# Moving a chunk's combining work on VectorE and ScalarE behind the next cell's normalisation

## The chip, the cores and the metric

The kernel runs on one core of a Trainium2 chip. Its time is the device time of one execution in microseconds (us), and a kernel's time is the median over its runs. A core has a matrix engine (PE, with its weight loads shown apart as PEld), a vector engine (DVE), a scalar engine (ACT), GpSimd (POOL) and a queue engine that issues DMAs (SP). Every engine works through its own instructions in the order in which the program wrote them, and waits for the others by semaphores.

## The reference

An mLSTM cell with exponential gating is followed by a two-layer block whose activation is h·cos(h). Everything is float32 on the chip (the two weight matrices come as float64).

```python
batch, n_heads, seq, head_dim = (4, 8, 768, 40)
n_tokens, d_model, d_ff = (3072, 320, 2048)

for t in range(S):                       # the cell, per batch b and head h
    m_new = max(f_gate + m, i_gate)
    f_stab, i_stab = exp(f_gate + m - m_new), exp(i_gate - m_new)
    C = f_stab * C + i_stab * outer(v, k);  n = f_stab * n + i_stab * k
    y[t] = sigmoid(o_gate) * (C @ q) / max(abs(n @ q), 1)
x = y.transpose(0, 2, 1, 3).reshape(B * S, H * D)     # 3072 x 320
h = x @ w_in                                          # 3072 x 2048
out = (h * cos(h)) @ w_out                            # 3072 x 320
```

## The kernel before

**Tiling.** The sequence is cut into NC = 6 chunks of 128 steps. A *cell* `n = c*B + b` is chunk c of batch b (B = 4, 24 cells). Within a cell the recurrence is done in parallel form: decays `E` (exponentials on ACT, L402), scores (`ps`, PE, L468), weighting (DVE, L474), values (`vt`, PE, L494 to L501), and a running state `st` between chunks. `turn_gate` (L446) and `normalize_turned` (L510 to L521) on DVE multiply by the output gate, divide by the normaliser and write the cell's columns of `xT`; `seam` (L569, L576) on PE then turns the last rows of that (`px`) and makes the state's update (`pu`).

The block works on one chunk of all four batches at a time, 512 tokens. Its 2048 hidden columns go in eight *slots* f2 = 0..7 of 2 x 128 columns. In a slot, PE makes `pup` (two PSUM banks, L611 and L614); ACT rounds it (`near`, L619), DVE takes the rest (L622), ACT makes the sine (L627), DVE makes the gated value `g` (`gate`, L631), and DVE and POOL form sums of quarters of `g` (`sums`, L680 to L688). Only two `pup` banks exist, so a slot's first matmul waits until the slot before it has been through `gate`.

From chunk 1 on the product with w_out uses a scheme with seven products in place of eight. Each chunk has four accumulators `acc` = X0, X1, Y0, Y1 in PSUM (pool `ps_o`, four banks in rotation). The last twelve products of chunk c-1 run in slot 0 of chunk c; the remaining two products per slot pair are kept as operands `D` and run in slot 1 of chunk c as `late`, 16 matmuls (32 records) that go into a fifth accumulator, which takes the bank that X0 had. `combine(c, p)` (L730 to L748) puts the accumulators together: for each p, one ACT copy of `X[:, 0]` into a scratch tile `m` (L737), then DVE additions (L738 to L748), and for p = 0 two output DMAs. `combine_late` (L750) adds `late` and sends the other two outputs. The scratch `m` has one buffer, shared (tag "db") with `db` of the normalisation; the second copy of a pair therefore waits for the additions that read the first.

**Order.** The program is written under a manual schedule: `both_parts(c, b)` (L924) writes two slots at a time, and each engine runs what it is given in that order. While the block works on chunk c, the cells of chunk c+1 run between its slots: in the first slot of a pair (i = 0) scores, weighting, decay of the next cell, values, normalisation; in the second (i = 1) `seam` and state. `down_slot` (L761) places the products. The end of a slot with i = 0 is `sin_next` (L914): a sine on a single element, which makes ACT load the table for sines ahead of the next slot. In slot 0 of a chunk `sigmoid` of the next chunk and `decay` stand on ACT ahead of that. `late_products` and `combine_late` stand in slot 1.

SP issues its DMAs in program order too: in slot 0 the two output DMAs of `combine`, and the load of a later cell's `E` (`load_E`, L351).

The slot 0 that matters is called the *seam of chunk c* below (c = 2, 3, 4). For c = 5 there is no next cell, so the block `if cell and i == 0` is skipped.

Of the kernel before, what the change touches and what calls it, by code (L numbers as in the profile page):

```python
# [29 lines left out]
def kernel(  # L30
# [430 lines left out]
    def scores(n):  # L461
        pool, tag = psum(n)
        qT, kT = qkT[n]
        ps = [pool.tile([128, HP, C], FP, name="ps", tag=tag) for _ in range(2)]
        for p in range(HP):
            for j in range(2):
                r = slice(64 * j, 64 * j + D)
                nc.tensor.matmul(ps[j][:, p], kT[r, p], qT[r, p], start=True, stop=True)  # L468
        pss[n] = ps
# [165 lines left out]
    def down(c, f2):  # L635
        if f2 == 0:
            po[c] = [ps_o.tile([128, DM], FP, name="po", tag="o") for _ in range(B)]

        order = [(f, b) for f in (2 * f2, 2 * f2 + 1) for b in range(B)]
        if f2 == NF // 2 - 1:  # L640
            order.sort(key=lambda fb: fb[1])
        for f, b in order:
            nc.tensor.matmul(po[c][b], gs[c, f][:, ts(b, C)], w_out_sb[:, f], start=(f == 0), stop=(f == NF - 1))  # L643
            if f == NF - 1:
                o = out_tile()
                nc.scalar.copy(out=o, in_=po[c][b])
                out_to(c, b, o)
# [5 lines left out]
    def out_tile():  # L653
        return po_s.tile([128, DM], FP, name="o_sb", tag="o_sb")

    def out_to(c, b, o):
        nc.sync.dma_start(out=out[b * S + c * C:b * S + (c + 1) * C], in_=o)
# [54 lines left out]
    def late_products(c):  # L712
        L = late[c] = ps_o.tile([128, 2, HALF], FP, name="late", tag="o")
        for k in range(NF // 2):
            for i, rhs in ((0, wv[:, k, 0, 1]), (1, wv[:, k, 1, 1])):
                yield L[:, i], Ds[c, k // 4][:, k % 4, i], rhs, k == 0 and i == 0, k == LAST and i == 1

    def run(made, n):
        for _ in range(n):
            a, lhs, rhs, start, stop = next(made)  # L720
            nc.tensor.matmul(a, lhs, rhs, start=start, stop=stop)  # L721

    def all_products(c):
        acc[c] = [ps_o.tile([128, 3, HALF], FP, name="acc", tag="o") for _ in range(4)]
        if c == NC - 1:
            late[c] = ps_a.tile([128, 2, HALF], FP, name="late", tag="a")
        for k in range(NF // 2):
            yield from products(c, k)

    def combine(c, p):  # L730

        X0, X1, Y0, Y1 = acc[c]
        X, Y, y = (X0, Y0, (0, 1)) if p == 0 else (X1, Y1, (0, 1))
        tt = nc.vector.tensor_tensor
        o = outs_of[c, p] = [out_tile() for _ in range(2)]
        s = p1.tile([128, 3 * C], FP, name="m", tag="db")
        nc.scalar.copy(out=s[:, 0:HALF], in_=X[:, 0])  # L737
        tt(out=o[0].rearrange("q (h n) -> q h n", h=2), in0=X[:, 1:3], in1=s[:, 0:HALF].unsqueeze(1).to_broadcast([128, 2, HALF]), op=OP.add)  # L738
        if p == 0:
            tt(out=s[:, HALF:DM], in0=Y[:, 0], in1=o[0][:, HALF:DM], op=OP.add)  # L740
            tt(out=o[1].rearrange("q (h n) -> q h n", h=2), in0=Y[:, 1:3], in1=s[:, HALF:DM].unsqueeze(1).to_broadcast([128, 2, HALF]), op=OP.add)
            tt(out=o[0][:, HALF:DM], in0=Y[:, 2], in1=o[0][:, HALF:DM], op=OP.add)
            tt(out=o[0][:, HALF:DM], in0=Y1[:, 2], in1=o[0][:, HALF:DM], op=OP.add)
            for e in range(2):
                out_to(c, e, o[e])
        else:
            tt(out=o[1][:, HALF:DM], in0=Y[:, 0], in1=o[0][:, HALF:DM], op=OP.add)
            tt(out=o[1][:, 0:HALF], in0=Y[:, 1], in1=o[1][:, HALF:DM], op=OP.add)  # L748

    def combine_late(c):  # L750
        tt = nc.vector.tensor_tensor
        o, L = outs_of[c, 1], late[c]
        tt(out=o[0][:, HALF:DM], in0=L[:, 0], in1=o[0][:, HALF:DM], op=OP.add)
        tt(out=o[1][:, HALF:DM], in0=L[:, 0], in1=o[1][:, HALF:DM], op=OP.add)
        tt(out=o[0][:, HALF:DM], in0=L[:, 1], in1=o[0][:, HALF:DM], op=OP.add)
        for e in range(2):
            out_to(c, 2 + e, o[e])
# [3 lines left out]
    def down_slot(c, f2):  # L761

        if c == 0:
            if f2 > 0:
                down(0, f2 - 1)
            return
        if f2 == 0:
            if c == 1:
                down(0, LAST)
            else:  # L770
                run(made_of[c - 1], 12)
                combine(c - 1, 0)
                combine(c - 1, 1)
            return
        if f2 == 1 and c > 1:
            run(late_products(c - 1), NF)
            combine_late(c - 1)
            return
        if c not in made_of:
            made_of[c] = all_products(c)  # L780
        each = 14 if c == NC - 1 else 12
        quota = [0] * 8
        for m in range(2, 8):
            quota[m] = each * 7 * (m - 1) // 6 - each * 7 * (m - 2) // 6
        run(made_of[c], each if c == 1 else quota[f2])
# [128 lines left out]
    def sin_next():  # L914

        nc.scalar.activation(out=spot, in_=spot, func=AF.Sin)
# [7 lines left out]
    def both_parts(c, b):  # L924

        n = (c + 1) * B + b
        cell = n < N
        for i in range(2):
            f2 = 2 * b + i
            up = Up(c, f2)  # L930
            if cell and i == 0:
                scores(n)
                if c == 0 and b == 0:

                    warm(8, psum_o())
            if cell and i == 1:
                seam(n)
                if n % 2 == 1 and n + 3 < N:
                    load_two(n + 3, "Kv")
            for e in range(2):  # L940
                up.near(e)
            for e in range(2):
                up.rest(e)
            if i == 0:
                if cell:
                    weigh(n)
                    if n + 1 < N:
                        decay_exponents(n + 1)
                for e in range(2):
                    up.sin(e)  # L950
                    up.gate(e)
                if c > 0:
                    sums(c, f2)
                if b == 0 and c + 1 < NC:
                    sigmoid(c + 1)

                if c == 0 and b > 0 and pieces:
                    to_float32(*pieces.pop(0))
                if cell and n + 1 < N and (c > 0 or b > 0):
                    decay(n + 1)  # L960
            else:
                if cell:
                    seam_out(n)
                if pieces:
                    to_float32(*pieces.pop(0))
                if cell:
                    state(n)
                for e in range(2):
                    up.sin(e)
                    up.gate(e)  # L970
                if c > 0:
                    sums(c, f2)
                while pieces:
                    to_float32(*pieces.pop(0))
                if cell and n + 1 < N:
                    weigh_k(n + 1)
                    odd_values(n + 1)
            down_slot(c, f2)
            if (c, f2) == (1, 0):
                weight_sums(1)  # L980
            if cell and i == 0:
                turn_gate(n)
                values(n)
                normalize_turned(n)
                fade(n)
                if n % 2 == 1 and n + 3 < N:
                    load_two(n + 3, "qk")
                if n + 3 < N:
                    load_E(n + 3)
                if b == B - 2 and c + 2 < NC:  # L990
                    load_o(c + 2)
                if c == 0 and b == 0:
                    next_out()
                    decay(n + 1)
                elif pieces:
                    to_float32(*pieces.pop(0))
                sin_next()
            if i == 1:
                if c == 0 and b + 2 < B:
                    pieces.extend(weights_in(b + 2))  # L1000
                for _ in range(min(2, len(outs))):
                    next_out()
                if (c, f2) == (0, LAST):
                    weight_sums(0)
                if cell and n + 1 < N:
                    turn_blocks(n + 1)
                    scale_q(n + 1)
# [41 lines left out]
```

## Time and profile before

| | us |
|---|---|
| three runs: median (lowest to highest) | 588.87 (586.77 to 594.44) |
| the profiled execution | 591.7 |
| its span, first to last instruction | 589.9 |
| PE busy | 548.5 (93%) |
| DVE busy | 421.3 (71%) |
| ACT busy | 279.4 (47%) |
| POOL busy | 219.6 (37%) |

The profile is of one execution. A timeline lists each engine's instructions with start and length in us from the start of the span, and in brackets the idle time before and what ended it. The chain follows the work that ended last back through what released each step. PEclk, in tables of stretches, is the share of the full PE clock that was granted. Matmuls of float32 appear as two records each ("x8" for four matmuls).

### The profile page before, as it was taken

The numbers are of one execution on the slowest core, as the hardware profiler recorded it, in microseconds if no ns is written. First come the engines' busy times: TensorE is split into PE (matmuls) and PEld (weight loads), VectorE is DVE, ScalarE is ACT, GpSimd is POOL, SyncE is SP. The second block draws the span as 40 slices with busy tenths as digits, with TensorE's granted clock in tenths as the row PEclk, the third lists the DMA queues.
The fourth block names the chain that finished last, engine by engine and source line by source line (L and its number), as shares of the span: only waits on it lengthen the run. The fifth ranks groups of instructions, "written<-read, shape, count | busy, mean of one in ns | idle before, by whom it ended". The sixth has DMA issues, their size and how long they took to land.

```text
span 589.9 us, 10485 instructions
## 1 busy us (share of the span) xinstructions
PE 548.5 (93%) x3884; PEld 370.1 (63%) x3884; DVE 421.3 (71%) x904; ACT 279.4 (47%) x549; POOL 219.6 (37%) x362
## 2 busy tenths in 40 slices
PE   8997959898999999969999969999969999999996
PEld 4883525555557576737676738667637667657665
DVE  3566797887677788767788766878776878676455
ACT  2665927385284365554265462465273462322211
POOL 7423362433396525415425323435312223122121
PEclk8778889797999999979999988999988999999999
DMA  9999999964615736515736615734710000010001
GB/s 153 220 227 191 235 240 231 198 179 89 117 46 121 122 81 146 62 58 112 117 81 125 83 58 109 120 82 90 117 59 23 2 1 2 1 45 1 0 1 44
DMA packets 126034, 58.85 MB, mean 100 GB/s; under 512 B 61808, under 2 KB 122304, under 8 KB 125984
## 3 DMA queue, kind: packets, MB, share of 16 engines
q1 hardware_dynamic: 125840, 58.00, 49.3%
q8 instruction: 30, 0.49, 0.4%
q14 instruction: 20, 0.16, 0.1%
q0 software_dynamic: 96, 0.18, 0.1%
q10 hardware_dynamic: 48, 0.02, 0.0%
HBM read 54.07 MB, written 5.16 MB: 100 GB/s over the span
## 4 chain that ended last, share of the span: by engine, by line
PE 72%; DVE 12%; ACT 7%; POOL 5%; DMA 2%; issue 2%; DVEq 0%; ACTq 0%; POOLq 0%; SPq 0%
PE pup L611 23%; PE acc L721 21%; PE pup L614 7%; PE late L721 4%; PE ps L468 4%; PE po L643 3%; ACT E L402 2%; PE vt L501 2%; PE vt L494 1%; DMA E<-M_d 1%; DVE t L441 1%; PE px L569 1%; DVE w_out_sb L154 1%; DVE n L622 1%; PE pt L431 1%
## 5 line engine op out<-in xcount | busy, mean ns | idle before, releaser
L611 PE MATMUL pup<-xT,w_in_sb 128*128 128x512 f32 x384 | 178.2, 607 | 2.0 <-POOL w_in_sb L157 1.1
L619 ACT ACTIVATE n<-pup 128x512 int32<-128x512 f32 x96 | 52.0, 592 | 228.0 <-PE pup L614 228.0
L622 DVE SCALAR_TENSOR_TENSOR n<-pup,n 128x512 f32<-128x512 f32 x96 | 61.8, 686 | 91.7 <-ACT n L619 91.7
L611 PEld LDWEIGHTS pup<-xT,w_in_sb 128*128 128x128 f32 x384 | 71.0, 193 | 78.4 <-issue 67.6
L685 POOL TENSOR_TENSOR D<-g 128x128 f32<-128x128 f32 x40 | 19.6, 490 | 249.1 <-DVE g L631 223.3
L627 ACT ACTIVATE n<-n 128x512 f32<-128x512 f32 x96 | 58.4, 630 | 15.6 <-DVE n L622 14.0
L631 DVE SCALAR_TENSOR_TENSOR g<-pup,n 128x512 f32<-128x512 f32 x96 | 61.7, 685 | 2.6 <-ACT n L627 1.4
L721 PE MATMUL acc<-w_out_sb,g 128*128 128x160 f32 x320 | 59.0, 305 | 0.0
L721 PE MATMUL acc<-T,g 128*128 128x160 f32 x320 | 58.2, 302 | 0.0
L614 PE MATMUL pup<-xT,w_in_l 64*128 64x512 f32 x192 | 54.2, 641 | 0.0
L402 ACT ACTIVATE E<-E,tab 128x128 f32<-128x128 f32 x160 | 49.0, 389 | 4.8 <-POOL E L388 4.6
L721 PEld LDWEIGHTS acc<-w_out_sb,g 128*128 128x128 f32 x320 | 47.4, 190 | 4.0 <-issue 2.3
L721 PEld LDWEIGHTS acc<-T,g 128*128 128x128 f32 x320 | 47.8, 190 | 2.3 <-issue 1.5
L643 PE MATMUL po<-w_out_sb,g 128*128 128x320 f32 x128 | 43.3, 499 | 0.7 <-POOL w_out_sb L157 0.7
L468 PEld LDWEIGHTS ps<-t,t 40*128 40x128 f32 x384 | 28.7, 215 | 20.6 <-issue 14.6
L468 PE MATMUL ps<-t,t 40*128 40x128 f32 x384 | 30.5, 306 | 9.8 <-DVE t L441 9.8
L614 PEld LDWEIGHTS pup<-xT,w_in_l 64*128 64x128 f32 x192 | 14.4, 184 | 36.4 <-issue 33.4
L643 PEld LDWEIGHTS po<-w_out_sb,g 128*128 128x128 f32 x128 | 27.5, 221 | 13.5 <-issue 4.7
L721 PE MATMUL acc<-T,S 128*128 128x160 f32 x160 | 35.2, 302 | 0.0
L474 DVE TENSOR_TENSOR E<-ps,E 128x512 f32<-128x512 f32 x48 | 30.8, 682 | 3.6 <-PE ps L468 3.6
L450 POOL TENSOR_TENSOR qG<-t,G 128x512 f32<-128x512 f32 x20 | 25.3, 1265 | 10.5 <-DVE t L441 10.4
L721 PE MATMUL acc<-w_out_sb,S 128*128 128x160 f32 x160 | 29.0, 300 | 0.0
(174 smaller groups left out, 904.5 us busy)
## 6 DMA issues: line engine op xcount, KB each, us to landing
E<-M_d SPq DMA_DIRECT2D x22, 512.0 KB, 6.1
qr<-in_q_dram SPq DMA_DIRECT2D x40, 160.0 KB, 3.7
kr<-in_k_dram SPq DMA_DIRECT2D x40, 160.0 KB, 5.4
G<-G_d SPq DMA_DIRECT2D x20, 256.0 KB, 6.0
bits<-in_moe_w_out_dram SPq DMA_DIRECT2D x8, 640.0 KB, 5.4
bits<-in_moe_w_in_dram SPq DMA_DIRECT2D x32, 128.0 KB, 4.1
out_dram<-o_sb SPq DMA_DIRECT2D x24, 160.0 KB, 1.8
o<-in_o_gate_dram SPq DMA_DIRECT2D x40, 80.0 KB, 4.0
```

Source lines behind the costliest of these rows:

```text
L402: nc.scalar.activation(out=Es[n][:, h], in_=Es[n][:, h], func=AF.Exp, scale=-1.0, bias=tab[:, c, 0, g:g + 1])
L450: nc.gpsimd.tensor_tensor(out=qG, in0=qkT[n][0], in1=Gs[n], op=OP.mult)
L468: nc.tensor.matmul(ps[j][:, p], kT[r, p], qT[r, p], start=True, stop=True)
L474: nc.vector.tensor_tensor(out=w, in0=pss[n][j], in1=w, op=OP.mult)
L611: nc.tensor.matmul(pu, w_in_sb[:, i, ts(2 * f2 + e, 128)], x(i), start=(i == 0), stop=False)
L614: nc.tensor.matmul(pu, w_in_l[r, f2], x(NK, r), start=False, stop=True)
L619: nc.scalar.activation(out=self.n[e], in_=self.pu[e], func=AF.Copy, bias=0.25)
L622: nc.vector.scalar_tensor_tensor(out=self.n[e].bitcast(FP), in0=self.pu[e], scalar=0.25, in1=self.n[e], op0=OP.add, op1=OP.subtract)
L627: nc.scalar.activation(out=r, in_=r, func=AF.Sin, scale=TWO_PI_DOWN)
L631: nc.vector.scalar_tensor_tensor(out=g, in0=self.pu[e], scalar=TWO_PI, in1=self.n[e].bitcast(FP), op0=OP.mult, op1=OP.mult)
L643: nc.tensor.matmul(po[c][b], gs[c, f][:, ts(b, C)], w_out_sb[:, f], start=(f == 0), stop=(f == NF - 1))
L721: nc.tensor.matmul(a, lhs, rhs, start=start, stop=stop)
```

## The change

The two calls of `combine` for the chunk before leave `down_slot`, where they stood right after the last twelve products, and go to the end of slot 0, behind `turn_gate`, `values`, `normalize_turned`, `fade`, `load_E` and `sin_next`. On DVE the eight additions so come after the normalisation; on ACT the two copies come after the table load and the one-element sine; on SP the two output DMAs come after the load of `E`. Nothing is added or taken out. For c = 5, where that block is empty, the order stays as it was.

```diff
@@ def down_slot(c, f2):
             else:
                 run(made_of[c - 1], 12)
-                combine(c - 1, 0)
-                combine(c - 1, 1)
             return
@@ def both_parts(c, b):
                 elif pieces:
                     to_float32(*pieces.pop(0))
                 sin_next()
+            if f2 == 0 and c > 1:
+                for p in range(2):
+                    combine(c - 1, p)
             if i == 1:
```

## The prediction

> **What bounds the kernel now.** I read the page's shares first, then the list of waits, then the chain around one chunk seam, then the timelines of the four engines there, and last the granted clock in short stretches.
>
> The chain by engine (page, part 4), and four lines of the list of waits (who waited for whom: us in all, times, longest):
>
> ```profile
> PE 72%; DVE 12%; ACT 7%; POOL 5%; DMA 2%; issue 2%; DVEq 0%; ACTq 0%; POOLq 0%; SPq 0%
> ```
>
> ```profile
> PE px L569 <- DVE xT L521: 18.1, 4, 5.9
> ...
> DVE o_sb L738 <- ACT m L737: 10.8, 4, 3.5
> ...
> ACT m L737 <- DVE o_sb L741: 9.0, 4, 4.3
> ```
>
> At the seams of chunks 2, 3 and 4 PE waits 5.88 us each time for the normalisation's last instruction; the rest of the first row is a wait of 0.5 earlier. In front of that DVE waits about 3.5 us for ACT's copy. The chain at the seam of chunk 2 (start, length, what; only the longer pieces):
>
> ```profile
> 251.73 2.45 ACT E L402 x8
> 254.18 0.18 ACT m L737
> ...
> 254.38 0.50 DVE o_sb L738
> ...
> 257.28 0.33 DVE o_sb L748
> 257.61 0.77 DVE oT L446
> ...
> 260.93 0.57 DVE xT L521
> 261.50 0.14 issue
> 261.63 0.77 PE px L569 x2
> 262.40 0.80 PE pu L576 x16
> 263.19 5.53 PE late L721 x32
> 268.72 3.43 PE pup L611 x8
> ```
>
> The reader sees a detour: PE → ACT (sigmoid, decay, copy) → DVE additions → DVE normalisation → PE. The normalisation has no need of the additions; it only stands behind them. Its own inputs are early: DVE is idle from 250.92 (end of `sums`), the gates `og` are there at 250.4, the values `vt` at 251.06.
>
> The idle time costs twice. The granted clock in four stretches (columns: stretch, length, busy of PE, PEld, DVE, ACT, POOL, clock, DMA):
>
> ```profile
> 255.60:261.60 6.00, 0.15 (x2) 0.00 (x0) 5.72 (x19) 2.73 (x5) 0.00 (x0) 0.73 0.45 143
> 261.60:263.20 1.60, 1.57 (x19) 1.27 (x19) 1.08 (x2) 0.77 (x3) 0.00 (x0) 0.50 0.00 0
> 263.20:268.70 5.50, 5.50 (x33) 5.50 (x34) 3.55 (x10) 0.55 (x2) 2.89 (x5) 0.82 0.00 0
> 268.70:272.10 3.40, 3.40 (x11) 1.21 (x9) 2.73 (x5) 0.00 (x0) 1.52 (x3) 1.00 0.37 117
> ```
>
> After the wait PE works at half clock for some us. The same work without a wait before it shows in two other rows: `px` and `pu` in the middle of a chunk, and `late` in chunk 5:
>
> ```profile
> 284.46 0.42 PE px L569 x2
> 284.88 0.47 PE pu L576 x16
> ```
>
> ```profile
> 521.54 4.54 PE late L721 x32
> ```
>
> So px+pu+late is 0.89+4.54 = 5.43 warm, against 7.10 here (+1.67); at the seams of chunks 3 and 4 the same sums give +2.69 and +1.45 (chunk 4 has no pu).
>
> **The change, step by step, at the seam of chunk 2.** Offsets come from the timelines of before.
>
> *DVE, normalisation.* turn_gate moves from 257.52 to 250.92, where `sums` end. By the row of xT (start 260.93, so 3.41 later) it starts at 254.33; px started 0.70 after that row, so px could start at 255.03. PE is busy with `pup` until 254.62+1.13 = 255.75. The 5.88 wait is gone, with 0.7 us to spare. The cover is that pup work; without it the normalisation would cost what it is late, us for us.
>
> *ACT.* Decay ends at 254.18. Now the table load and the one-element sine come first: from that load to the next instruction took 1.40 (256.25 to 257.65), so the first copy runs at 255.60 instead of 254.08. The scratch `db` it overwrites is read by xT until 254.9, so that is no wait.
>
> *DVE, additions.* L738 follows its copy by 0.30: 255.90, done 256.39. L741 0.96 later: 256.86. Second copy 0.60 after that: 257.46. L743 ends and the second L738 starts at 257.92; 1.12 later (256.40 to 257.52) the queue is free: 259.04. The additions now stand in front of `rest` of slot 1. `near` stands behind the second copy on ACT: 257.75, the pair done at 258.80, so DVE decides: rest at 259.04 (before: 261.40), +1.20; state +0.90 (pu ready long before); gate at 261.14, its first half done at 261.83. Before, gate started at 264.22.
>
> *PE.* px and pu from 255.75 to 256.64. `late` takes X0's bank; X0's last reader is L738, done 256.39, so `late` starts without a wait. That release is a wait which before never ended last; it counts from the same L738. With `late` warm, PE is free at 261.18. The next `pup` needs the first gate: 261.9. So a new wait of 0.7 stands where 5.88 stood, and `pup` of slot 2 starts 6.8 earlier than 268.72.
>
> *What is late next.* Behind the gates DVE has sums (1.32 to their start, 1.49 long), combine_late (0.70) and two transposes for the next scores (2.03): done 266.68. PE ends `pup` at 261.9+4.49 = 266.39, so the scores wait about 0.35. Before, DVE had 2.38 idle after those transposes; that reserve is spent here, but from the next slot on DVE waits for ACT again and PE runs on.
>
> *POOL and SP.* POOL has no instruction moved; its sums wait for the gates, earlier. On SP the E load passes ahead of the two output DMAs; its buffer is free since `vt` (251), and nobody waits for these outputs for a chunk. I cost both at nothing; the cover is the 90 us between seams.
>
> *Sum.* Chunk 2: 6.8-0.35 = 6.45. Chunk 3 lies 90.07 later in all rows, but its late took longer: pup at 359.82, 1.03 more, so 7.48. Chunk 4 (181.16 later) has no pu and no state: late 256.45 to 260.99, gate 260.40 to 261.09, pup 261.15 against 449.20-181.16 = 268.04, 6.89; but its sums take 2.11, the transposes end at 266.66 and PE at 265.64, a wait of 1.05: 5.84. Chunk 5: no change. Together 19.8. Against the profiled execution, 591.7: 571.9. That execution was 2.8 over the median of the runs shown; nothing in the saving hangs on that part, so from 588.87 I predict 569.1.
>
> **Bounds.** No new wait at all: 7.54, 8.57 and 7.33, 23.4 in all, 565.4. Cold clock as now in spite of the shorter waits: 5.8 less, 13.9, 575.0. I take the warm rows, since the trace has one wait of PE of just this kind and size, `pup` for `g` L631, 0.9 us, early in chunk 1, and the stretch around it (180 to 200) shows a clock of 1.00.
>
> A rule that speaks against this: the Trainium skill, "TensorE: Matmul & The Clock Gate", section "A second HAM failure mode: psum-queue depth-cycling", says that frequent short idles between groups of matmuls can make the clock fall back. If the waits of 0.7 and 0.35 did that, the sum would be the 13.9 just given; the row of 180 to 200 says otherwise.
>
> Normalisation now runs beside POOL's sums and fade, where POOL had been idle. In the middle of a chunk the same stretch, beside the fade (POOL, 279.60 to 281.03), took from 279.70 to 283.67, 3.97; at the seam without POOL 257.52 to 261.49, 3.97. I cost it at nothing, and 0.7 us of slack covers it.
>
> "GPSIMD Engine Reference" in the Trainium skill, section "Specifications", says that GpSimd shares its SBUF interfaces with VectorE and contends with instructions of two SBUF inputs. Of the normalisation only the last product is one; by the rule its 0.56 could double, which still fits in the slack.
>
> **Rivals.**
>
> *PSUM released late.* If the first `late` matmul waits for the whole of combine (259.04) and not for L738, late ends at 263.65: savings 5.07, 6.10, 4.39, together 15.6, time 573.3. For it: no row of before shows that wait. Against: X0 has only L737 and L738 as readers. With a cold `late` on top (1.0 to 2.0 a seam, 4.1 in all): 577.4.
>
> *The wait moves to ACT.* Copies now stand between the sine's table load and `near`. If they made ACT load a table again, three loads of 1.28 on the way to the gate, `pup` would start 3.84 later: 19.8-11.5 = 8.3 saved, 580.6, no measurable change. Against: in chunk 5 the copy L737 (516.11) follows sines directly, with no load between.
>
> *Slower: the clock.* The seams are the only pauses that PE has between 200 and 575 us. If continuous work made the granted clock fall below 1.00, the 330 us that follow the first seam, all bound by PE, would grow: below a mean of 330/(330+19.8) = 0.943 the kernel is slower than before; at 0.90 it adds 37, 606. Against: from 449 to 575 PE ran 126 us without a pause at 1.00.
>
> *The change does not do what it says*, because normalisation waits for something that the additions hid: og and vt are there 0.5 us ahead of their readers or earlier, so I see no candidate.
>
> **Chances.** Forecast 0.72; late release 0.10; cold clock kept 0.06; no gain (ACT, or a wait not seen) 0.08; slower 0.04. No change, as far as this kernel's measurement can tell, is within 2%, here 577.1 to 600.6. Faster 0.72+0.10+0.06 = 0.88, same 0.08, slower 0.04. The range goes from 563 (the bound 565.4 less the 2 us by which the fastest run lies under its median) to 578 (late release with a cold clock, 577.4).
>
> **What would show it.** After: px with no idle time ahead of it at three seams; `xT` about 6.6 us earlier than the additions allow now; PEclk 1.00 through `late`, at about 4.54 us; `pup` of slot 2 waiting 0.7 or less for `g` L631; scores waiting a few tenths for the transposes. The prediction is wrong if `late` starts after the last addition, if a table load stands ahead of L737, or if PEclk falls elsewhere.

## The result and the profile after

| | before | after |
|---|---|---|
| median, us (lowest to highest, 4 runs each) | 589.01 (586.77 to 594.44) | 572.38 (568.36 to 573.04) |
| profiled execution, us | 591.7 | 573.04 |
| its span, us | 589.9 | 571.3 |
| PE busy | 548.5 (93%) | 542.4 (95%) |
| DVE busy | 421.3 (71%) | 420.8 (74%) |
| first `pup` of chunk 1 to the start of the last row of `late` | 402.59 | 383.15 |

The ratio is 0.969, with a 95% interval of 0.961 to 0.977: faster. The last row of the table leaves out the first 180 us, which come out differently in every execution; more on that below. Among the runs of the experiments one (571.58 us, "second group later") counts as slow, over 1.5% above the fastest of its kernel, and is left out of that kernel's median and ratio.

PE's waits after, between 180 and 575 us (who waited for whom: us in all, times, longest):

```profile
PE pup L611 <- DVE g L631: 2.0, 3, 0.9
PE ps L468 <- DVE t L441: 0.8, 1, 0.8
PE late L721 <- DVE o_sb L738: 0.3, 1, 0.3
```

The three waits of 5.9 us for `xT` are no longer in the list. In their place stand short ones: `pup` for the gates, the scores for the transposes, and, once, `late` for the addition that frees its bank. (One of the three pup waits, 0.9, lies early in chunk 1 and was there before.)

The chain at the seam of chunk 2, after (start, length, what). Everything here starts 0.82 us later than in the trace of before, since `pup` of slot 1 ends at 256.57 and not at 255.75:

```profile
252.56 2.44 ACT E L402 x8
...
256.51 0.18 ACT m L737
...
256.72 0.50 DVE o_sb L738
...
259.72 1.28 DVE n L622 x2
...
261.81 0.70 DVE g L631
262.51 0.04 issue
262.56 3.70 PE pup L611 x8
266.26 1.06 PE pup L614 x4
267.32 0.10 issue
267.42 1.16 PE ps L468 x16
```

The normalisation has left the chain. What ends last now is decay, the table load with its one-element sine, the first copy behind them, the additions, `rest`, state and the first gate; from there on it is PE. On PE's own timeline px, pu and late follow each other without a gap:

```profile
256.49 0.49 PE L569 MATMUL px<-xT,pick 128*128 128x128 f32 x2
256.91 0.54 PE L576 MATMUL pu<-vs,kw 128*40 128x48 f32 x16
257.38 4.61 PE L721 MATMUL late<-w_out_sb,D 128*128 128x160 f32 x32
```

No idle time in brackets, and `late` takes 4.61 where it took 5.60. The clock in the stretch that answers to the four shown of before (same columns, the clock is third from the right):

```profile
256.50:262.50 6.00, 5.50 (x52) 5.08 (x50) 5.55 (x16) 2.85 (x8) 0.00 (x0) 1.00 0.15 55
```

### The profile page after: what moved, and what is told of

Its sections match the earlier page's. It is cut to its first block, busy times and chain, and to the rows that moved or that the text cites. A ratio compares the mean times of both kernels' runs of the same rounds, so it can differ in the third digit from the quotient of the medians.

```text
span 571.3 us, 10482 instructions
## 1 busy us (share of the span) xinstructions
PE 542.4 (95%) x3884; PEld 364.2 (64%) x3884; DVE 420.8 (74%) x904; ACT 279.7 (49%) x549; POOL 220.4 (39%) x362
## 4 chain that ended last, share of the span: by engine, by line
PE 66%; DVE 10%; DMA 6%; ACT 5%; SPq 5%; POOL 5%; issue 2%; ACTq 0%; DVEq 0%; POOLq 0%
PE pup L611 23%; PE acc L721 22%; PE pup L614 7%; PE po L643 4%; PE ps L468 3%; PE vt L501 2%; PE vt L494 2%; DVE n L622 1%; PE late L721 1%; DVE t L441 1%; DMA bits<-in_moe_w_out_dram 1%; ACT E L402 1%; DVE g L631 1%; SPq L141 1%; DMA o<-in_o_gate_dram 1%
## 5 line engine op out<-in xcount | busy, mean ns | idle before, releaser
L611 PE MATMUL pup<-xT,w_in_sb 128*128 128x512 f32 x384 | 176.1, 600 | 4.9 <-POOL w_in_sb L157 2.6
L388 POOL TENSOR_SCALAR_AFFINE_SELECT E<-E 128x1024 f32<-128x1024 f32 x22 | 24.1, 1096 | 9.6 <-DVE E L387 9.6
```

The lines of the kernel that those rows point to most:

```text
L388: nc.gpsimd.affine_select(out=E, in_=E, compare_op=OP.is_ge, fill=1.0e30, base=0, pattern=[[0, H], [1, C]], channel_multiplier=-1)
L611: nc.tensor.matmul(pu, w_in_sb[:, i, ts(2 * f2 + e, 128)], x(i), start=(i == 0), stop=False)
```

## Experiments

All times are medians against the kernel before on the same chip. As the first 180 us scatter, each run's *inner time* is given too, taken from its profile: from the first `pup` of chunk 1 to the start of the last row of PE's timeline, four records of `late`. It comes from one execution of each kernel; the two kernels that were profiled more than once repeat it to 0.04 us.

| kernel | median, us | before, same chip | ratio (95%) | inner time |
|---|---|---|---|---|
| before, second profile | 588.33 (one) | 591.70 | | 402.55 |
| dummy matmuls in the wait | 587.25 | 591.70 | 0.991 (0.987 to 0.995) | 396.82 |
| half of the move | 588.77 | 591.70 | 0.996 (0.993 to 0.999) | 399.14 |
| after, second profile | 567.99 (one) | 591.70 | | 383.14 |
| after, beside the variants | 574.99 | 592.06 | 0.970 (0.961 to 0.978) | 383.12 |
| combine ahead of the sine | 572.86 | 592.06 | 0.968 (0.960 to 0.977) | 383.58 |
| scratch of their own | 568.05 | 592.06 | 0.960 (0.951 to 0.968) | 379.62 |
| second group later | 565.21 | 592.06 | 0.957 (0.948 to 0.967) | 379.48 |

The second and the third row lie within 2% of before, so by their times they count as the same; what they show is read from the inner time and the traces. The last four rows are faster than before.

### What the idle time costs beside itself

The kernel before, with PE kept busy in the wait:

```diff
             if cell and i == 1:
+                if f2 == 1 and c > 1:
+                    warm(24, ps_a.tile([128, HP, C], FP, name="wm", tag="a"))
                 seam(n)
```

> The kernel before, with 24 dummy matmuls of zeros (128x512, bfloat16; into a free PSUM bank, nothing reads them) on PE ahead of seam at chunks 2, 3 and 4, to fill the 5.88 us wait. The order of the additions is as before, so the wait for the normalisation stays. At the pace of the dummy matmuls in the trace of before (8 from 53.90 to 55.78, 0.215 to 0.235 us each) they take some 5.2 us. Theory (the idle time costs twice, 5.88 of wait and 1.5 to 2.7 of half clock after it): clock 1.00 in late, px+pu+late 5.4 us in place of 5.9 to 8.1 us, the time 4 to 6 us below before, about 584. Rival (late is long for another reason, such as its operands or the release of a bank): late keeps its 5.5 to 6.6 us and the time stays within 1 us of before, or rises if the dummy matmuls run past the normalisation.

Measured: inner time 396.82, so 5.77 us less, with the normalisation as late as ever; the median is 4.45 below that of before, 587.25 against 591.70 (4 to 6 below was expected; the "about 584" was missed, as before itself took longer on this chip than the 588.87 shown ahead of the prediction). PE at the first seam (with the idle time before, and its releaser):

```profile
258.36 5.35 PE L792 MATMUL wm<-nil 128*128 128x512 bf16 x24
264.36 0.46 PE L569 MATMUL px<-xT,pick 128*128 128x128 f32 x2 [0.64 <-DVE xT L521]
```

and the clock in that stretch and the next:

```profile
258.40:264.30 5.90, 5.32 (x26) 2.23 (x24) 5.62 (x19) 2.73 (x5) 0.00 (x0) 1.00 0.46 146
264.30:269.70 5.40, 5.34 (x51) 5.19 (x52) 4.66 (x12) 1.31 (x3) 1.80 (x4) 1.00 0.00 0
```

The clock stays at 1.00, px runs in 0.46 where it took 0.77, and late takes 4.61 at the first two seams and 4.51 at the third. So of the 19.4 us that the change saves, 5.8 are the slow clock after the wait; the rest, 13.7, is the three waits, 17.6, less what the new short ones cost. The rival (late is long by its operands or its bank) falls.

### Half of the move

```diff
                 combine(c - 1, 0)
-                combine(c - 1, 1)
             return
@@ end of slot 0
                 sin_next()
+            if f2 == 0 and c > 1:
+                combine(c - 1, 1)
```

> Half of the change: the first group of additions (p = 0) stays ahead of the normalisation, only the second (p = 1, one copy and three additions) goes to the end of slot 0. Theory (the normalisation only stands behind the additions in the DVE queue, so each addition moved gives its own time): the wait of px falls by the second group's 1.12 us, from 5.88 to 4.8, the clock still falls in it, and the time is about 3.4 us below before, 585 to 586. Rival (the saving hangs on the point at which ACT's copies stand, ahead of or behind the table load): the second copy is behind the sine here, so most of the saving of 17 us would come already with this half.

Measured: inner time 3.45 us less than before, where about 3.4 was expected; the median is 2.9 less, ratio 0.996. PE's waits between 195 and 575 us:

```profile
PE px L569 <- DVE xT L521: 14.2, 3, 4.7
```

Three waits of 4.7, not 5.9: the three additions that left the queue ahead of the normalisation took away just their own length, and the place of the second copy behind the sine did nothing more. The clock still fell (late took 6.25, 5.84 and 6.09). The rival, by which half of the move brings most of the saving, falls; the saving is a matter of what stands ahead in DVE's queue.

### Two second profiles

> The kernel before once more, for a second profile. Theory on the missing part of the saving (19.8 forecast, 16.6 between the medians): the profiled execution of before was a slow one by 2.8 us, in its waits for input in the first 180 us or in the clock after the seams, and the forecast subtracted a saving of that execution from a median of others. Then this profile shows px waits of 5.88 again, and px+pu+late at the three seams that differ by 1 us or more from the 7.10, 8.12 and 6.41 of the first, or another length of the first 180 us. Rival: the saving at a seam was sized wrongly; then both are the same as in the first profile.

> The changed kernel once more, for a second profile. Theory (seams have no clock loss left, what varies is the first 180 us): the distance from the first pup of chunk 1 to that of slot 2 at each seam and to the end repeats within 0.3 us, and only the first 180 us differ. Rival (the new short waits at the seams are chance): the waits of pup and of the scores differ by more than 0.5 us from the 0.56, 0.9 and 0.8 of the first profile.

Measured: the inner times repeat, 402.55 (402.59) and 383.14 (383.15). Before, `late` took 5.58, 6.62 and 5.85 at the three seams against 5.60, 6.62 and 5.86 in the first profile; after, the pieces from the end of `pup` to the next `pup` are 5.99, 5.99 and 5.26 against 5.99, 5.98 and 5.26. What differs is where chunk 1 begins: its first `pup` starts at 181.65 and 178.34 in the two profiles of before, at 182.46, 177.42 and (in the run beside the variants) 184.42 in the three of after. So the seams were sized rightly. Of the two places in which the extra time of before's first profile might have lain, it was not the clock after the seams; it was the first 180 us. The rivals of both runs fall.

> The changed kernel beside the three variants on one chip. Theory: from the first pup of chunk 1 to the last matmul 383.1 us as in both profiles so far, 19.4 below the 402.6 of before; the ratio of the times 0.967, since the first 180 us differ from run to run in both kernels alike. Rival: another chip gives other waits at the seams, and that time differs by more than 1 us.

On another chip the inner time is 383.12 and the ratio 0.970 (0.961 to 0.978): the theory holds.

### What the new short waits come from

First, combine behind the normalisation but ahead of the sine (this and the next two edits are against the changed kernel):

```diff
+                if f2 == 0 and c > 1:
+                    for p in range(2):
+                        combine(c - 1, p)
                 sin_next()
-            if f2 == 0 and c > 1:
+            if f2 == 0 and c > 1 and not cell:
```

> The changed kernel, with combine still behind the normalisation on DVE but ahead of the one-element sine and its table load on ACT. Theory (the first copy waits for the normalisation's last read of the shared scratch, 254.9 on the clock of the first profile of before, then the table load of 1.28 and the sine of 0.2 stand between the second copy and near): near comes at 258.5, its first half done at 259.1, against 259.04 when DVE is free, so rest and the gates shift by under 0.2 us and the time from the first pup of chunk 1 to the last matmul stays within 0.5 us of the 383.15 of the changed kernel. Rival (the table load ahead of the copies is what the new waits of pup come from): the first copy comes 1.4 us earlier, the waits of pup (0.56, 0.56 and 0.30 at the three seams) go, and that time falls by 1.4 to 3.

Measured: inner time 383.58, 0.4 more than after. ACT at the seam of chunk 2:

```profile
251.43 0.29 ACT L737 COPY m<-acc 128x160 f32<-128x160 f32 x1 [0.71 <-DVE xT L521]
253.24 0.29 ACT L737 COPY m<-acc 128x160 f32<-128x160 f32 x1 [1.52 <-PE pu L576]
253.55 1.28 ACT L914 ACT_TABLE_LOAD   x1
254.85 0.20 ACT L914 ACTIVATE spot<-spot 1x1 f32<-1x1 f32 x1
254.96 1.05 ACT L619 ACTIVATE n<-pup 128x512 int32<-128x512 f32 x2
```

The first copy waits for `xT`, since it overwrites the scratch that the normalisation reads, and the second waits for the first group's additions (L741 ended at 253.13; the trace names pu, which ended at about that time). Then the table load delays `near` in place of the copies. The waits of `pup` did not go, as the rival had it; they are 0.69, 0.69 and 0.65 here. (Of the 0.56, 0.56 and 0.30 that this expectation and the one on the second group name for the changed kernel, the last is not a wait of `pup`: at chunk 4 its trace has 0.27 us of `late` waiting for L738, and `pup` follows without a pause.) So the order of sine and copies makes 0.4 us in all, as long as the copies and the normalisation share one scratch buffer. So I gave them others: the first copy a tile of its own, the second a buffer of `kw` that is free at that time.

```diff
-        s = p1.tile([128, 3 * C], FP, name="m", tag="db")
-        nc.scalar.copy(out=s[:, 0:HALF], in_=X[:, 0])
+        if p == 0:
+            s = p1.tile([128, 3 * C], FP, name="mi", tag="db")
+            m = p1.tile([128, HALF], FP, name="m", tag="m")
+        else:
+            m = p2.tile([128, H, 64], FP, name="mk", tag="kw").rearrange("p h d -> p (h d)")[:, 0:HALF]
+        nc.scalar.copy(out=m, in_=X[:, 0])
```

> As the run with combine ahead of the sine, and in addition the two ACT copies write to scratch tiles of their own, so that neither waits for the normalisation nor for the additions of the first group. Theory (what delays rest at the seam is the chain from copy to copy over the shared scratch): copies at 254.2 and 254.5 on the clock of the first profile of before, additions without a pause from 254.9 to 258.04, near done by 257.2, rest 1.0 us earlier than in the changed kernel; pup and late wait no more, the scores wait under 0.5 us at chunk 4, and the time from the first pup of chunk 1 to the last matmul falls by about 2.6 us from 383.15, to 380.5. Rival (the gates are bound by ACT's sines or by the length of DVE's queue as such): under 1 us.

Measured: inner time 379.62, 3.5 us less than after (2.6 expected), with the same order as the run before, which took 383.58; so 3.96 is the scratch buffers. The rival (under 1 us) falls. Both copies run right behind decay, and `rest` follows the additions without a pause. All that is left of PE's waits between 195 and 560 us:

```profile
PE ps L468 <- DVE t L441: 0.4, 1, 0.4
```

The other way to the same end leaves the scratch alone and moves more of DVE's queue out of the way:

```diff
-                for p in range(2):
-                    combine(c - 1, p)
+                combine(c - 1, 0)
+                if not cell:
+                    combine(c - 1, 1)
@@ down_slot, slot 1
-            combine_late(c - 1)
+            if c == NC - 1:
+                combine_late(c - 1)
@@ end of slot 1
                     turn_blocks(n + 1)
                     scale_q(n + 1)
+                if cell and f2 == 1 and c > 1:
+                    combine(c - 1, 1)
+                    combine_late(c - 1)
```

> The changed kernel, with the second group of additions (p = 1, with its copy) and combine_late moved further, behind the transposes at the end of slot 1 (chunk 5 as before). Theory (in the changed kernel DVE's queue of slot 1 is what the seam still waits for: 1.12 us of the second group stand ahead of the gates, and 1.12 + 0.70 us ahead of the transposes): gates 1.1 us earlier, so pup of slot 2 waits no more (0.56, 0.56, 0.30), transposes 1.8 us earlier, so the scores wait no more (about 0.37, 0.37 and 1.05, some of it as slower matmuls); the time from the first pup of chunk 1 to the last matmul falls by about 3 us from 383.15, to 380.2. Rival (the accumulators then come free too late for the products of slot 2, which take the same banks): acc in slot 2 waits for L738 or L755 and the gain is under 1 us or negative.

Measured: inner time 379.48, 3.64 us less than after (about 3 expected); the median is 565.21 against 574.99 of the changed kernel on the same chip, of which part is the scatter of the first 180 us. DVE at the seam of chunk 2:

```profile
254.16 0.32 DVE L743 TENSOR_TENSOR o_sb<-acc,o_sb 128x160 f32<-128x160 f32 x1
254.40 1.28 DVE L622 SCALAR_TENSOR_TENSOR n<-pup,n 128x512 f32<-128x512 f32 x2
```

and PE in the chain of the same kernel:

```profile
253.26 4.54 PE late L721 x32
257.80 3.43 PE pup L611 x8
262.29 0.89 PE ps L468 x16
```

`rest` stands right behind the first group; late, pup and scores have no wait at this seam, and pup and scores their short lengths (3.43 and 0.89, against 3.70 and 1.16 in the chain of after). That is where both variants gained more than I had added up: a group of matmuls that starts late costs 0.27 us besides its wait. By the timelines 0.16 of that is the overlap with the end of the work before, which it loses (`pup` of before starts at 268.56, while `late` ends at 268.72), and 0.10 is its own length (3.70 against 3.60). The accumulators come free in time, so the rival falls. One wait of 0.3 stays, late for L738 at chunk 4. Of the versions run this and the one with scratch tiles have the shortest inner times; between the two the runs cannot tell. By their medians alone they are not told from the changed kernel either, since the intervals of the ratios overlap; that they beat it is read from the inner times.

## Why the prediction was right

The forecast was 569.1 us in a range of 563 to 578; measured 572.38.

*The normalisation's wait.* Forecast: gone, with 0.7 us to spare. Measured: `xT` starts at 255.08 (255.15 by the forecast with the offset of 0.82) and px has no idle time before it. Right. That it ran in its old time beside POOL's sums and fade is right too: 251.66 to 255.64, 3.98, against 3.97. But L521, the one product whose 0.56 us the prediction let double by the rule that it cites, did not run beside POOL: it started at 255.08, and POOL's fade had ended at 253.81. So its 0.56 us here say nothing on that rule, and neither does the row from the middle of a chunk, where the fade ended at 281.03 and the normalisation at 283.67.

*ACT and the additions.* Forecast with the offset: first copy 256.42, rest 259.86, gate 261.96, pup 262.72. Measured: 256.42, 259.72, 261.81, 262.56. The difference is that some of the additions followed each other a little faster.

*The seams.* From the end of `pup` to the next `pup` the three seams lost 6.8, 7.8 and 6.9 us, where 6.8, 7.83 and 6.89 were forecast. Together 21.5; of that 2.1 is given back by `pup` and scores that run slower and scores that wait, where I had 0.35, 0.35 and 1.05, 1.75 in all. The inner time so fell by 19.4 against 19.8.

*The clock.* Forecast: 1.00 through late. Measured: 1.00 in every stretch of after from 182 us to the last matmul. The short waits of 0.3 to 0.9 us left it alone. What "TensorE: Matmul & The Clock Gate" in the Trainium skill says of frequent short idles between groups ("A second HAM failure mode: psum-queue depth-cycling") did not show in any run here; but one or two waits in 84 us are few, so this is no test of frequent ones.

*The rivals.* Late release of the bank: `late` waits for L738, as the forecast had it, by 0.3 once. A further table load among the copies: none stands there, the one ahead of the sine is all. A clock that falls under continuous work: not seen. POOL and SP at nothing: between 182 and 566 us no wait of an engine in the trace of after names a DMA, and none of PE names POOL.

*What was off: 3.3 us of the time.* The mechanism held; the step that was off is the last one, from the profiled execution to the median: "nothing in the saving hangs on that part, so from 588.87 I predict 569.1". The profiled executions bear out 573.04 against a forecast of 571.9, and that rest is 0.8 us of a later chunk 1 and 0.35 of scores. But medians of four runs of each kernel differ by 16.6 us. The first 180 us alone spread over some 7 us in the profiles (177.4 to 184.4), enough for 2.8 us between two sets of four runs; that it was this in the runs without a profile is likely, not shown. The ratio's interval, 0.961 to 0.977 of 589, is a saving of 13.5 to 23 us and holds the 19.4. What makes the first 180 us vary was not tried. The traces show what goes with it: over the first 177 us the mean granted clock is 0.90, 0.87 and 0.83 in the three profiles of after, in which chunk 1 starts at 177.42, 182.46 and 184.42. Whether the clock is the cause there or follows from other waits is open.

## What to carry to other kernels

Read a wait of the busiest engine through to the instruction it waits for, and then ask what that instruction itself needs: here it needed nothing of the 3.1 us of additions ahead of it in the queue, nor of the 3.5 us for which they waited for ScalarE, so its place alone cost 5.9 us a seam. An idle matrix engine can cost more than the gap: here three waits of 5.9 us cost 5.8 more, since PE came back at half clock, while waits of up to 0.9 us did not lower the clock. And after such a move the same additions stand ahead of something else: look at what is next in that queue, and at scratch buffers that two engines share, before calling it done.

## What the runs showed of the hardware

In the first profile of before PE runs dry at 255.75 us, the granted clock falls from 1.00 to 0.50 at 258.34, PE starts again at 261.63 and the clock is back at 1.00 at 265.17. So it fell 2.6 us after PE ran dry and came back 3.5 us after the work had begun again; at the seams of chunks 3 and 4 these are 4.7 and 5.6, and 2.3 and 3.3 us. With waits of 4.7 us (half of the move) it fell after 2.8, 1.9 and 4.9 us, the last time when PE was already at work again.

The clock stood at 0.50 for 6.83 us at each of the three seams of before, for 6.83, 6.83 and 3.41 in half of the move, and at 1.00 for 85.33 and 81.92 between the seams of before: its changes lie on steps of 3.41 us. So it hangs on where the end of PE's wait falls among these steps how much of the work runs at half clock. In before it was 3.5, 5.6 and 3.3 us; half of each is 1.8, 2.8 and 1.6, close to the 1.67, 2.69 and 1.45 by which px, pu and late were longer. The two profiles of before, whose chunks lie 3.31 us apart, show the same `late` at each seam to 0.04 us; as 3.31 is nearly one step, this agreement may be chance.

Matmuls of zeros that nobody reads, in a wait of 5.9 us, were enough to keep the clock at 1.00.
